# Twelve of 103 zero fills moved from GpSimd's DMA queue to SyncE's in an attention-and-FFN training step

## The chip, the cores and the metric

The kernel runs on one core of one Trainium2 chip. The metric is device time in microseconds (us), the median of several runs.

The engines are PE (matmul), DVE (VectorE), ACT (ScalarE), POOL (GpSimd) and SP (SyncE). SP only issues DMAs here. POOL issues DMAs too, through a queue that the profile calls "software_dynamic"; those of SP and ACT are "hardware_dynamic".

## The reference, cut to what matters

One decoding step and its gradient: layer norm, attention of one query over the last 4096 rows of a 32768-row cache (8 key/value heads), a residual, a second layer norm, a bilinear gated FFN. The outputs are the result and the gradients of all inputs.

```python
W = min(4096, max(256, Sk // 4))              # 4096 of Sk = 32768 rows are used
k = jnp.repeat(k_cache[:, :, Sk - W:, :], rep, axis=1)
v = jnp.repeat(v_cache[:, :, Sk - W:, :], rep, axis=1)
...
g = x @ w_gate;  u = x @ w_up;  h = g * u;  return h @ w_down
...
_out, _vjp = jax.vjp(_f, A_x, A_k_cache, A_v_cache, ...)   # gradients of the whole caches
```

Only 4096 of 32768 rows are used, so seven eighths of the two cache gradients are zeros. They must be written all the same: 224 MiB of zeros. 206 MiB of them are 103 writes of 2 MiB, the "fills" of this text. The other 18 MiB go out on SP's queue late in pass 2 and at the end.

## The kernel before: what the change touches

The kernel has three stages. Pass 1 goes over the eight heads (scores, softmax, moments) and loads K and V. The middle holds the output projection `wo`, the FFN and its gradient, in three blocks of weights. Pass 2 goes over the heads again and writes the gradients of K and V.

The 103 fills go out on POOL's queue. They read one SBUF area, `zeros`. Its upper half is lent to block 1 of the FFN weights in between, and this makes three kinds of fill:

- `HALF0` fills read the full width of `zeros`. Block 1's weights may be loaded only when all of these have finished.
- Fills `HALF0` to `HALF1` read the lower half twice, so they may go on while block 1's weights lie in the upper half.
- The rest must wait until block 1 is done and the upper half has been set to zero again (below called *the memset*).

```python
HALF0, HALF1 = 42, 63
zeros = ar(0, ZW)                              # ZW = 8192 columns, all 128 partitions
wgu_off = [RB + 28 * KB, ZW // 2]              # block 1's w_gate, w_up: upper half of zeros
# ... cut ...
def send_fills(n0, n1, halves=False):
    for reg in fills[n0:n1]:
        if halves:
            ZQ.dma_start(out=reg.rearrange("p (k f) -> p k f", k=2), in_=zeros[:, 0:ZW // 2].unsqueeze(1).to_broadcast([128, 2, ZW // 2]))
        else:
            ZQ.dma_start(out=reg, in_=zeros)

send_fills(0, HALF0)
send_fills(HALF0, HALF1, True)
# ... cut: pass 1, with its loads of K and V ...
after = {0: [("K", 3), ("V", 3)], 1: [("K", 4), ("V", 4), ("K", 5)], 2: [("V", 5)], 3: [("V", 6), ("K", 6)], 4: [("K", 7)], 5: [("V", 7)]}
# ... cut: wo in two halves, load_wo(0) in pass 1, load_wo(1) behind it; then load_block(0), load_block(1) ...
for n in range(len(BLOCKS)):
    # ... cut: the FFN block's compute ...
    if n + 2 < len(BLOCKS):
        load_block(n + 2)
    if n == 1:
        nc.vector.memset(ar(ZW // 2, ZW // 2), 0.0)     # "the memset"
        send_fills(HALF1, len(fills))
```

One thing must be known about the language: the order of instructions on an engine's queue is not the order of the program text. The build reorders them, keeping the dependences. SP's loads of V3, V4 and V5 (V3 is the V of head 3), for example, go out at 26 to 35 us, long before the place where the text has them. `tc.issue_after(x)` pins what it encloses behind `x` on the same engine, but says nothing about how far behind.

## Time and profile before

| | before |
|---|---|
| time, median of 3 runs | 803.09 us (802.88 to 803.20) |
| span of the profiled run | 802.6 us |
| busiest compute engine | PE, 57% of the span |
| moved by DMA | 334.84 MB, mean 417 GB/s |
| pass 1 ends (`wo`'s second half can be issued) | 299.5 us |
| the memset | 375.1 to 376.8 us |
| last compute | 720.6 us |

The page cuts the span into 40 slices. Here are its row of DMA business (in tenths; 9 is 90% or more) and the rate in each slice.

```profile
DMA  9999999999999999999999999999999999999993
GB/s 354 430 430 431 429 428 430 429 429 429 428 424 425 425 419 403 420 423 426 428 421 412 429 430 429 427 428 427 426 425 425 425 425 424 422 408 423 429 438 171
```

The DMA engines have no gap in 39 of 40 slices. The table of windows gives the same in numbers: stretch in us, its length, busy time of each engine with its number of instructions, the granted TensorE clock, the DMA share, GB/s.

```profile
350.00:370.00 20.00, 6.53 (x48) 3.91 (x48) 5.34 (x18) 1.29 (x4) 2.00 (x3) 0.50 1.02 422
370.00:380.00 10.00, 2.03 (x5) 0.57 (x6) 9.48 (x22) 0.00 (x0) 1.33 (x2) 0.50 1.01 428
380.00:390.00 10.00, 3.09 (x20) 2.06 (x19) 7.08 (x13) 2.52 (x5) 1.33 (x2) 0.50 1.01 429
390.00:400.00 10.00, 3.74 (x13) 2.99 (x13) 6.65 (x25) 0.00 (x0) 1.21 (x2) 0.50 1.01 427
...
720.00:770.00 50.00, 0.00 (x0) 0.00 (x0) 0.56 (x1) 0.39 (x1) 0.00 (x0) 0.50 1.01 426
770.00:790.00 20.00, 0.00 (x0) 0.00 (x0) 0.00 (x0) 0.00 (x0) 0.00 (x0) 0.50 0.93 401
790.00:803.00 13.00, 0.00 (x0) 0.00 (x0) 0.00 (x0) 0.00 (x0) 0.00 (x0) 0.50 0.17 74
```

Two readings matter. First, the middle of the kernel, where compute waits most, still has a DMA share of 1.01. Second, the end: after 720 us no compute is left, and in the last 13 us the share is 0.17. The 16 DMA engines do not finish together.

The chain of work that ended last reads thus:

```profile
PE 35%; DMA 32%; DVE 16%; ACT 4%; issue 2%; another core or an unknown queue 0%; SPq 0%; ACTq 0%; DVEq 0%
```

It names PE first, but it follows waits of instructions back from the last one. It can't say that 16 engines were full throughout. The DMA row says it.

SP's own instructions near the end of pass 1, in order of time (start, length; merged instructions of one kind show the time from the first to the end of the last):

```profile
248.13 0.33 SPq L196 DMA_DIRECT2D arena<-in_A_v_cache_dram  x1
260.67 0.57 SPq L352 DMA_DIRECT2D arena<-in_B_w_gate_dram  x1
278.95 0.34 SPq L321 DMA_DIRECT2D arena<-in_A_wo_dram  x1
292.02 1.62 SPq L353 DMA_DIRECT2D arena<-in_B_w_down_dram  x2
299.52 0.33 SPq L321 DMA_DIRECT2D arena<-in_A_wo_dram  x1
300.39 15.55 SPq L351 DMA_DIRECT2D arena<-in_B_w_gate_dram  x2
316.00 1.16 SPq L352 DMA_DIRECT2D arena<-in_B_w_gate_dram  x1
```

V7 is loaded at 248, the two halves of `wo` at 279 and 299.5. Then SP stands still: the second w_gate load in the line at 300.39 is block 1's and waits until 315.4 for the last full-width fill.

### The profile page before, as it was taken

The page shows a single profiled execution, that of the slowest core. Times are in us where ns is not written, and L with a number is a line of the kernel's source. Part 1 is how long each engine was busy: PE and PEld are TensorE (multiplying, and loading weights), DVE is VectorE, ACT ScalarE, POOL GpSimd, SP SyncE. Part 2 cuts the span into 40 slices and gives each one's busy share as a digit, 9 for nine tenths or more (in the row PEclk, how much of TensorE's full clock was granted, in tenths as well). Part 3 has the DMA queues.
Part 4 walks back from the last instruction along what each step waited for, and adds up shares of the span by engine and source line. Part 5 has one row for each costly group of instructions (what it writes and reads, how often), then busy time and mean ns, then how long its engine had stood idle before and what let it go on. Part 6 is the DMA issues. An engine that isn't in the chain of part 4 may idle for free.

```text
span 802.6 us, 8458 instructions
## 1 busy us (share of the span) xinstructions
PE 460.6 (57%) x3157; PEld 247.8 (31%) x3180; DVE 368.5 (46%) x1173; ACT 196.1 (24%) x309; POOL 63.6 (8%) x112
## 2 busy tenths in 40 slices
PE   0469999999999992622329397645263054630000
PEld 0334554545645551311219143322122012200000
DVE  2026264463462652255680876766691175860000
ACT  0143314223224000000002045543341034540000
POOL 4000000010100100011110010000000000000000
PEclk9989999999999997555559689776557557655555
DMA  9999999999999999999999999999999999999993
GB/s 354 430 430 431 429 428 430 429 429 429 428 424 425 425 419 403 420 423 426 428 421 412 429 430 429 427 428 427 426 425 425 425 425 424 422 408 423 429 438 171
DMA packets 29103, 334.84 MB, mean 417 GB/s; under 512 B 2819, under 2 KB 5638, under 8 KB 6918
## 3 DMA queue, kind: packets, MB, share of 16 engines
q0 software_dynamic: 17520, 216.01, 63.7%
q1 hardware_dynamic: 10102, 116.68, 34.7%
q10 hardware_dynamic: 1440, 1.61, 0.6%
q8 instruction: 25, 0.41, 0.2%
q14 instruction: 16, 0.13, 0.0%
HBM read 53.69 MB, written 280.59 MB: 416 GB/s over the span
## 4 chain that ended last, share of the span: by engine, by line
PE 35%; DMA 32%; DVE 16%; ACT 4%; issue 2%; another core or an unknown queue 0%; SPq 0%; ACTq 0%; DVEq 0%
DMA out_dram<-arena 17%; PE M_ps L311 10%; PE ok_ps L315 6%; PE rows_ps L255 6%; PE tr_ps L252 4%; DMA dh_bc<-in_grad_out_dram 4%; DMA arena<-in_A_k_cache_dram 4%; DMA arena<-in_A_wo_dram 3%; ACT arena L269 2%; DVE arena L640 2%; DVE arena L641 2%; DVE arena L452 2%; PE dqb_ps L495 2%; DMA arena<-in_B_w_up_dram 2%; DMA arena<-in_B_w_gate_dram 2%
## 5 line engine op out<-in xcount | busy, mean ns | idle before, releaser
L307 DVE TENSOR_SCALAR arena<-arena,p_f 128x256 bf16<-128x256 bf16 x512 | 109.9, 284 | 66.9 <-PE M_ps L311 35.7
L311 PE MATMUL M_ps<-arena 128*128 128x512 bf16 x489 | 120.1, 380 | 1.4 <-issue 0.2
L255 PE MATMUL rows_ps<-arena,vpad 128*16 128x512 bf16 x256 | 86.0, 430 | 23.3 <-DVE arena L603 16.8
L252 PE MATMUL tr_ps<-ident_bf,arena 128*128 128x128 bf16 x1024 | 88.5, 237 | 15.3 <-DMA arena<-in_A_k_cache_dram 9.5
L252 PEld LDWEIGHTS <-arena 128*128 128x128 bf16 x1024 | 66.3, 105 | 65.5 <-issue 54.9
L132 POOL DMA_DIRECT2D out_dram<-arena x82 | 45.1, 550 | 522.2 <-DMA out_dram<-arena 506.3
L269 ACT COPY arena<-tr_ps 128x1024 bf16<-128x1024 bf16 x64 | 61.8, 1015 | 88.6 <-PE tr_ps L252 88.6
L633 PE MATMUL d_ps<-arena,rT 32*128 32x512 bf16 x256 | 44.4, 507 | 63.1 <-DVE arena L641 37.6
L311 PEld LDWEIGHTS <-arena 128*128 128x128 bf16 x512 | 46.2, 99 | 50.8 <-issue 6.5
L315 PE MATMUL ok_ps<-arena 128*16 128x256 bf16 x512 | 57.5, 273 | 0.9 <-DVE arena L296 0.9
L601 ACT COPY arena<-tr_ps 128x1024 bf16<-128x1024 bf16 x32 | 32.5, 1016 | 97.7 <-PE tr_ps L252 40.4
L637 ACT CAST arena<-d_ps 128x512 bf16<-128x512 f32 x64 | 37.6, 587 | 69.5 <-PE d_ps L633 69.5
L640 DVE CAST arena<-d_ps 128x512 bf16<-128x512 f32 x64 | 44.0, 687 | 14.5 <-PE d_ps L633 14.3
L315 PEld LDWEIGHTS <-arena 128*16 128x16 bf16 x512 | 45.4, 90 | 13.9 <-issue 3.4
L641 DVE CAST arena<-d_ps 128x512 bf16<-128x512 f32 x64 | 43.6, 681 | 7.3 <-DMA out_dram<-arena 7.3
L638 ACT CAST arena<-d_ps 128x512 bf16<-128x512 f32 x64 | 38.1, 595 | 6.8 <-DMA out_dram<-arena 6.8
L633 PEld LDWEIGHTS <-rT 32*128 32x128 bf16 x256 | 11.2, 95 | 90.5 <-issue 58.2
L255 PEld LDWEIGHTS <-vpad 128*16 128x16 bf16 x256 | 19.1, 91 | 56.7 <-issue 49.1
L318 ACT COPY arena<-M_ps 128x512 f32<-128x512 f32 x16 | 8.6, 589 | 75.0 <-PE M_ps L311 75.0
L507 DVE CUSTOM_DVE_ANT_0 arena<-arena 128x4096 bf16<-128x4096 bf16 x3 | 13.1, 4423 | 24.3 <-ACT arena L500 24.3
L603 DVE COPY arena<-tr_ps 128x1024 bf16<-128x1024 bf16 x32 | 21.7, 682 | 3.7 <-PE tr_ps L252 3.7
L130 POOL DMA_DIRECT2D out_dram<-arena x21 | 14.0, 666 | 114.3 <-DMA out_dram<-arena 114.3
(196 smaller groups left out, 368.5 us busy)
## 6 DMA issues: line engine op xcount, KB each, us to landing
out_dram<-arena POOLq DMA_DIRECT2D x103, 2048.0 KB, 55.3
out_dram<-arena SPq DMA_DIRECT2D x18, 2048.0 KB, 33.3
arena<-in_A_v_cache_dram SPq DMA_DIRECT2D x10, 2048.0 KB, 49.9
arena<-in_A_k_cache_dram SPq DMA_DIRECT2D x8, 2048.0 KB, 29.4
out_dram<-arena SPq DMA_DIRECT2D x4, 4096.0 KB, 58.8
arena<-in_A_wq_dram SPq DMA_DIRECT2D x2, 3072.0 KB, 14.8
arena<-in_A_wo_dram SPq DMA_DIRECT2D x2, 1792.0 KB, 17.8
out_dram<-arena SPq DMA_DIRECT2D x2, 1792.0 KB, 32.6
```

The source lines that it names most:

```text
L132: ZQ.dma_start(out=reg, in_=zeros)
L252: nc.tensor.transpose(tr_ps[:, dh, i, :], X_sb[:, 4 * q + i, dh * 128:(dh + 1) * 128], ident_bf[:])
L255: nc.tensor.matmul(rows_ps[:], lhsT=pad[:, dh, 16 * q:16 * q + 16], rhs=XT[:, dh].rearrange("p t k -> p (t k)"), start=(q == 0 and dh == 0 ...
L269: sT_ps = dots(kv_at(K_off[g]), KT_slot, vpad[g % 2], rows1, ps_c, "cols", lambda q, XT, ps: nc.scalar.copy(out=XT, in_=ps))
L307: nc.vector.tensor_scalar(out=pK[:, i, hh, :], in0=K_sb[:, t, :], scalar1=p_f[:, 8 * i + c, hh:hh + 1], scalar2=None, op0=ALU.mult)
L311: nc.tensor.matmul(M_ps[:, vh, :], lhsT=V_sb[:, t, vh * 128:(vh + 1) * 128], rhs=pK[:, i, :, :].rearrange("p h d -> p (h d)"), start=(t == ...
L315: nc.tensor.matmul(ok_ps[:, k, :], lhsT=ppad[g % 2][:, 8 * (t % 4) + t // 4, :], rhs=X_sb[:, t, :], start=(g == 0 and k == 0 and t == 0), ...
L633: nc.tensor.matmul(d_ps[:, qi].rearrange("p w d -> p (w d)"), lhsT=rT[32 * q:32 * (q + 1), :], rhs=RB_[32 * q:32 * (q + 1), l, :], start=T ...
L637: nc.scalar.copy(out=stV[:, t:t + 2, :], in_=d_ps[:, :, 0, :])
L638: nc.scalar.copy(out=stK[:, t:t + 2, :], in_=d_ps[:, :, 1, :])
L640: nc.vector.tensor_copy(out=stV[:, t:t + 2, :], in_=d_ps[:, :, 0, :])
L641: nc.vector.tensor_copy(out=stK[:, t:t + 2, :], in_=d_ps[:, :, 1, :])
```

## The change

The intent, as far as the diff tells it: have the full-width fills done sooner, so that block 1's weights can come sooner, and keep the DMA engines fed by putting single fills into SP's queue behind loads that have slack.

```diff
-HALF0, HALF1 = 42, 63
+HALF0, HALF1 = 32, 46
+SYNC = 12
...
+    own = fills[len(fills) - SYNC:]
+    fills = fills[:len(fills) - SYNC]
+    def fills_behind(ins, n):
+        with tc.issue_after(getattr(ins, "ins", ins)):
+            for _ in range(n):
+                LD.dma_start(out=own.pop(), in_=zeros)
...
         after = {0: [("K", 3), ("V", 3)], ...}
+        behind = {2: 2, 3: 2, 4: 2, 5: 3}
...
+            if g in behind:
+                fills_behind(ins, behind[g])     # ins: the last load of K or V issued for g
...
     def load_block(n):
         for eng, i, wt in ((LD, 0, B_w_gate), (nc.scalar, 1, B_w_up)):
-            (rows 0 to 383, then rows 384 to 447)
+            (rows 384 to 447, then rows 0 to 383; load_block returns SP's last w_gate load)
...
-            if n + 2 < len(BLOCKS):
-                load_block(n + 2)
+            if n == 0:
+                last = load_block(2)
             if n == 1:
                 nc.vector.memset(ar(ZW // 2, ZW // 2), 0.0)
                 send_fills(HALF1, len(fills))
+                fills_behind(last, 3)
```

Fills that may go ahead of the memset: 63 before; 46 on POOL and 9 on SP after, 55 together. Behind it: 40 before; 45 on POOL and 3 on SP after.

More of the change, by code (lines that the diff above doesn't have):

```diff
@@ L195, in load_kv @@
     def load_kv(off, cache, g):
-        LD.dma_start(out=kv_at(off), in_=cache[0, g, Sk - W:, :].rearrange("(p t) d -> p t d", t=T))
+        return LD.dma_start(out=kv_at(off), in_=cache[0, g, Sk - W:, :].rearrange("(p t) d -> p t d", t=T))
     load_kv(K_off[0], A_k_cache, 0)
@@ L332 @@
                 if kind == "K":
-                    load_kv(K_off[n], A_k_cache, n)
+                    ins = load_kv(K_off[n], A_k_cache, n)
                 else:
-                    load_kv(V_off[n], A_v_cache, n)
+                    ins = load_kv(V_off[n], A_v_cache, n)
+            if g in behind:
+                fills_behind(ins, behind[g])
             if g == G - 2:
@@ L350, in load_block @@
         for eng, i, wt in ((LD, 0, B_w_gate), (nc.scalar, 1, B_w_up)):
-            eng.dma_start(out=wgu[:, 0:3, i, :], in_=wt[0:384, :].rearrange("(p c) f -> p c f", c=3)[:, :, f0:f0 + w])
             eng.dma_start(out=wgu[0:DQ, 3, i, :], in_=wt[384:D, f0:f0 + w])
+            ins = eng.dma_start(out=wgu[:, 0:3, i, :], in_=wt[0:384, :].rearrange("(p c) f -> p c f", c=3)[:, :, f0:f0 + w])
+            if eng is LD:
+                last = ins
         LD.dma_start(out=wd, in_=B_w_down[f0:f0 + w, :].rearrange("(p b) n -> p b n", b=nb))
+        return last
     load_block(0)
```

## The prediction

> **What bounds the kernel now.** The DMA engines, from beginning to end. The page's slices show DMA at 9 tenths in 39 of 40 slices, and the table of windows gives a DMA share of 0.99 to 1.02 in every stretch from 5 us to 770 us. 334.84 MB are moved; at the 428 GB/s of the window 20:300 that is 782 us of the 802.6 us span. The other 20 us are the start (221 GB/s in the first 5 us), slower mixed traffic (404 GB/s at 300:320, 416 at 420:450), and the end, where the engines finish one after another (401 GB/s at 770:790, 74 in the last 13 us). No compute engine is busy over 57%, and after 720 us only DMA runs.
>
> **What the change does.** It moves no byte fewer. 63 fills could be sent by GpSimd before the late memset; now 46 can, plus 9 on SyncE: 55. After it: 45 on GpSimd and 3 on SyncE, instead of 40. The Trainium skill, page "DMA: Bandwidth & Descriptors", section "Issuing engines are not separate DMA queues", says that queues of all issuing engines run on the same 16 DMA engines. This trace agrees: GpSimd's fills come every 4.9 to 5.1 us when alone and every 9.7 us beside SyncE's loads, with 428 GB/s either way. So moving fills should buy almost nothing directly. Packets of 16 KB take 618 ns on average in the software queue and 614 ns in SyncE's: on 12 fills of about 5 us, some 0.4 us.
>
> **Indirect effects.**
> 1. Block 1's FFN weights overwrite the upper half of the zeros, so their loads wait for the full-width fills: SyncE waits 13.6 us there, 301.7 to 315.3, and ScalarE's w_up load goes only at 327.7. With 32 + 9 full fills rather than 42, this wait should mostly go; the FFN gets some 10 us shorter.
> 2. V5's load is issued already at 35 us, far ahead of the program's place. The two fills behind it then stand before K3's load, which landed at 122.7, when PE needed it. Two fills at 9.7 us each: K3 lands at about 142, pass 1 ends about 18 us later (near 317 instead of 299.5).
> 3. Net, the late memset comes at about 385 instead of 376.8. By 376.8 the DMA had completed 53.6 fills, by 385 it could have completed 55.3; only 55 exist. So the DMA may run dry for a few us near 385.
>
> Compute ending 10 us later costs nothing; only idle DMA costs: 0 to 5 us, against a gain of about 1 us.
>
> **Prediction.** 802.5 us; 797 to 810 holds it 8 times in 10. Faster by over 2%: 0.02. Within 2%: 0.94. Slower by over 2%: 0.04.
>
> **What would show it.** DMA share still about 1.01 in all windows, except perhaps a dip near 375 to 392; PE idle some 18 us before the scores that need K3 (near 123 us) and pass 1 ending near 317; SyncE's wait for GpSimd's fills before block 1's load shorter than 5 us; last compute between 715 and 740; the end still staggered over some 15 us.
>
> **What would make it wrong.** If the fills run out well before the memset (a longer delay of pass 1, or SyncE's fills holding up the wo and FFN loads), each idle us of DMA costs one us: 15 us or more would make it slower by over 2%. If the staggered end comes from software-issued fills on one slow DMA engine, fewer of them could save up to 5 us. If the fills behind V5 are issued only later, pass 1 is not delayed and nothing runs dry.

## The result, and the profile after

| | before | after |
|---|---|---|
| time, median (4 runs each) | 802.99 us (801.63 to 803.20) | 812.67 us (812.12 to 813.48) |
| span of the profiled run | 802.6 us | 810.3 us |
| pass 1 ends (`wo`'s second half can be issued) | 299.5 us | 319.1 us |
| the memset | 375.1 to 376.8 us | 394.1 to 395.9 us |
| last compute | 720.6 us | 738.6 us |

The ratio is 1.0125, with a 95% interval of 1.0107 to 1.0143. A ratio here is the mean time of one kernel's runs over that of the other's of the same rounds, so it is not quite the ratio of the medians. The change made the kernel 1.2% slower. That is below 2%, but clear of noise, and outside the predicted range (797 to 810 us).

The same rows of the page, after:

```profile
DMA  9999999999999999998499999999999999999997
GB/s 358 427 432 427 429 431 428 430 431 429 428 423 429 411 426 423 419 425 361 180 425 392 426 436 427 425 428 425 422 429 420 426 422 430 421 420 405 439 432 332
```

There is a hole in slices 19 and 20 (361 and 180 GB/s), and the last slice is fuller than before (332 instead of 171 GB/s). The windows:

```profile
350.00:370.00 20.00, 11.78 (x96) 8.18 (x93) 9.50 (x23) 1.80 (x5) 0.00 (x0) 0.58 1.01 425
370.00:380.00 10.00, 2.85 (x8) 0.72 (x8) 4.92 (x16) 1.29 (x4) 0.00 (x0) 0.50 1.02 422
380.00:390.00 10.00, 3.69 (x40) 3.19 (x40) 1.20 (x2) 0.00 (x0) 0.00 (x0) 0.50 0.24 95
390.00:400.00 10.00, 2.02 (x5) 0.56 (x6) 9.48 (x25) 0.87 (x1) 3.62 (x7) 0.50 0.33 131
...
720.00:770.00 50.00, 7.17 (x37) 1.76 (x37) 12.89 (x27) 9.18 (x17) 0.00 (x0) 0.52 1.01 419
770.00:790.00 20.00, 0.00 (x0) 0.00 (x0) 0.00 (x0) 0.00 (x0) 0.00 (x0) 0.50 1.01 432
790.00:800.00 10.00, 0.00 (x0) 0.00 (x0) 0.00 (x0) 0.00 (x0) 0.00 (x0) 0.50 0.99 426
800.00:811.00 11.00, 0.00 (x0) 0.00 (x0) 0.00 (x0) 0.00 (x0) 0.00 (x0) 0.50 0.54 229
```

Between 380 and 400 us the DMA share is 0.24 and 0.33. POOL shows why, in its instructions in order of time:

```profile
342.79 0.67 POOL L131 DMA_DIRECT2D out_dram<-arena  x1 [9.31 <-DMA out_dram<-arena]
396.19 1.08 POOL L133 DMA_DIRECT2D out_dram<-arena  x2 [52.72 <-DVE arena L443]
```

POOL sent the last fill it was allowed at 342.8 and stood still for 52.7 us until the memset (L443 of the changed kernel) was done. What had been queued was finished near 382, but for a few packets.

To put a number on it I took starts and durations of all DMA packets in the trace. At each moment, idle is 16 minus the packets in flight (not below zero), over 16. Summed up to the last packet this is the mean idle time of one DMA engine:

| mean idle per DMA engine, us | start (to 20 us) | middle | end (from 750 us) | sum | span | span minus sum |
|---|---|---|---|---|---|---|
| before | 2.0 | 0.1 | 9.9 | 11.9 | 802.6 | 790.7 |
| after | 2.1 | 14.3 | 2.7 | 19.2 | 810.3 | 791.2 |

The last column is the same within half a microsecond: the fills cost the same DMA time in either queue. The 7.7 us between the spans are 14.3 us more idle in the middle, less 7.1 us that came back at the end; the rest is rounding, the start and that half microsecond. The end is less ragged because in the dry stretch the engines that were behind could catch up: at 384 to 389 us never more than 3 packets of fills were in flight, leftovers of engines that were behind, while the others waited. The landings show it too. Each fill reports its landing in 16 parts, and I take the time from the first part to the last as a measure of how far apart the engines are. It was 11.2 us for the fill that POOL sent at 376.8 in the kernel before, and 0.8 us for its first fill behind the dry stretch after the change. For the last transfer on SP's queue it was 16.4 us before and 5.7 us after.

So two questions are left: why was the memset 19 us later, and is it this lateness, through the dry engines, that cost the time?

**Where the 19 us arise.** PE's list in order of time holds one long wait in pass 1 that the kernel before does not have at that place:

```profile
172.19 1.89 PE L261 MATMUL tr_ps<-ident_bf,arena 128*128 128x128 bf16 x16 [18.40 <-DMA arena<-in_A_k_cache_dram]
```

PE waited 18.4 us for a load of K. Which one, SP's list shows:

```profile
34.61 0.33 SPq L205 DMA_DIRECT2D arena<-in_A_v_cache_dram  x1
90.01 0.33 SPq L205 DMA_DIRECT2D arena<-in_A_k_cache_dram  x1
90.43 0.95 SPq L141 DMA_DIRECT2D out_dram<-arena  x2
91.43 0.60 SPq L205 DMA_DIRECT2D arena<-in_A_v_cache_dram  x1
117.84 3.82 SPq L205 DMA_DIRECT2D arena<-in_A_k_cache_dram  x2
```

The fills pinned "behind V5" (34.61) were put by the build behind K3's load (90.01). K3 still landed at 122.4. The line at 117.84 holds two loads: K5, which goes to the place of V1, at 117.8, and K4, which goes to the place of K1 and had to wait for that, at 121.3. Both stood behind two fills more than before. By the semaphores in the trace K4 landed at 172.2, where PE's wait ends; in the kernel before it landed at 152.2, and PE did not wait for it. SP's queue had been full since the start, at half of the bandwidth, so a 2 MiB fill took some 9.7 us (POOL's fills came every 9.7 us then): two of them, 19.4 us, against 20.0 us by which K4 came later and 18.4 us of PE's wait. The Trainium skill, page "DMA: Bandwidth & Descriptors", section "Queues, rings and completion order", says that on each DMA engine descriptors are consumed in ring order. This trace agrees: what SP issued from 90 us on landed in the order of issue, K3 at 122.4, the fills at 132.6 and 142.7, then a V at 152.6, K5 at 162.4 and K4 at 172.2.

**The FFN was not shortened.** From the end of pass 1 to the memset's start it took 75.6 us before (299.5 to 375.1) and 75.0 us after (319.1 to 394.1). SP again, after:

```profile
267.72 0.34 SPq L205 DMA_DIRECT2D arena<-in_A_v_cache_dram  x1
268.10 4.59 SPq L141 DMA_DIRECT2D out_dram<-arena  x3
280.27 26.15 SPq L363 DMA_DIRECT2D arena<-in_B_w_gate_dram  x2
306.47 1.29 SPq L364 DMA_DIRECT2D arena<-in_B_w_gate_dram  x1
307.87 1.43 SPq L330 DMA_DIRECT2D arena<-in_A_wo_dram  x1
311.63 1.75 SPq L367 DMA_DIRECT2D arena<-in_B_w_down_dram  x2
319.13 0.33 SPq L330 DMA_DIRECT2D arena<-in_A_wo_dram  x1
```

Block 1's w_gate load now stands *ahead* of the first half of `wo`. It waits, until 305.9, for the last full-width fills. These were the three that SP itself had put behind V7: the last of them landed at 305.8, POOL's last full-width fill at 284.3. And `wo` waits behind the load. `wo`'s first half went out at 307.9, 11 us before the end of pass 1; in the kernel before it went out 20.6 us before it. In the projection PE waited for `wo` twice:

```profile
330.24 6.00 PE L391 MATMUL ao_ps<-arena,oX_bf 128*1 128x448 bf16 x16 [8.27 <-DMA arena<-in_A_wo_dram]
345.68 5.12 PE L391 MATMUL ao_ps<-arena,oX_bf 128*1 128x448 bf16 x16 [9.44 <-DMA arena<-in_A_wo_dram]
```

Before, it was once:

```profile
303.49 3.19 PE L376 MATMUL ao_ps<-arena,oX_bf 128*1 128x448 bf16 x16 [1.13 <-DVE oX_bf L373]
320.06 5.76 PE L376 MATMUL ao_ps<-arena,oX_bf 128*1 128x448 bf16 x16 [13.38 <-DMA arena<-in_A_wo_dram]
```

What block 1's earlier weights gained was given back by the later `wo`. The last matmul of the projection ended at 350.8, 31.7 us after the end of pass 1, against 26.3 us before (325.8); from there to the memset it took 43.3 us instead of 49.3. So 5.4 us were lost and 5.9 won.

### The profile page after: what moved, and what is told of

The parts are those of the page before. It is cut to its first block, busy times and chain, and to the rows that moved or that the text cites. A ratio compares the mean times of both kernels' runs of the same rounds, so it can differ in the third digit from the quotient of the medians.

```text
span 810.3 us, 8485 instructions
## 1 busy us (share of the span) xinstructions
PE 463.4 (57%) x3180; PEld 247.5 (31%) x3180; DVE 368.5 (45%) x1173; ACT 196.2 (24%) x309; POOL 55.6 (7%) x100
## 4 chain that ended last, share of the span: by engine, by line
DMA 35%; another core or an unknown queue 26%; DVE 14%; PE 9%; issue 4%; POOL 2%; ACT 1%; SPq 0%; DVEq 0%; ACTq 0%; POOLq 0%
DMA out_dram<-arena 35%; DVE arena L656 3%; DVE arena L657 2%; DVE arena L468 2%; PE dqb_ps L511 2%; PE rows_ps L264 2%; DVE arena L549 1%; DVE arena L642 1%; PE d_ps L649 1%; PE tr_ps L261 1%; POOL out_dram L133 1%; DVE arena L438 1%; DVE arena L523 1%; POOL out_dram L131 1%
## 5 line engine op out<-in xcount | busy, mean ns | idle before, releaser
L320 PE MATMUL M_ps<-arena 128*128 128x512 bf16 x512 | 123.6, 383 | 0.0
L133 POOL DMA_DIRECT2D out_dram<-arena x77 | 41.7, 544 | 516.7 <-DMA out_dram<-arena 463.7
L264 PEld LDWEIGHTS <-vpad 128*16 128x16 bf16 x256 | 18.7, 90 | 57.0 <-issue 49.3
L391 PE MATMUL ao_ps<-arena,oX_bf 128*1 128x448 bf16 x32 | 11.1, 532 | 17.7 <-DMA arena<-in_A_wo_dram 17.7
```

The costliest lines, as they stand in the source:

```text
L264: nc.tensor.matmul(rows_ps[:], lhsT=pad[:, dh, 16 * q:16 * q + 16], rhs=XT[:, dh].rearrange("p t k -> p (t k)"), start=(q == 0 and dh == 0 ...
L320: nc.tensor.matmul(M_ps[:, vh, :], lhsT=V_sb[:, t, vh * 128:(vh + 1) * 128], rhs=pK[:, i, :, :].rearrange("p h d -> p (h d)"), start=(t == ...
```

## The experiments

The theory after reading the trace: the memset is late, the 55 fills run out first, and only the dry DMA engines cost time. Rivals: fills on SP cost as such (1); late compute costs as such (2); 55 fills ahead of the memset are simply too few (3). All seven kernels gave correct results. Two cautions on the expectations. Where they say "K3" of the late load (e1, e3, e5, e6), it was K4. And the "Rival 2" in e1's text is another one: that `wo` behind block 1's load makes the memset late. Each ratio compares with runs of the kernel before in the same rounds.

### e1: the two fills pinned behind V5 given back to POOL

```diff
-HALF0, HALF1 = 32, 46
-SYNC = 12
+HALF0, HALF1 = 34, 48
+SYNC = 10
-        behind = {2: 2, 3: 2, 4: 2, 5: 3}
+        behind = {3: 2, 4: 2, 5: 3}
```

> Theory (the DMA engines run dry because the FFN's memset comes 19 us late, and K3 behind two fills is what makes it late): without the two fills behind V5 (GpSimd sends them, so 55 fills before the memset as in the changed kernel) K3 lands near 123 us, PE does not wait for it, pass 1 ends at 299 to 302 us, the memset ends at 376 to 382 us, when 53.6 to 54.6 of the 55 fills are done; the DMA is dry for 0 to 3 us; 801 to 804 us. Rival 1 (SyncE's fills as such cost, by their packets or by SyncE's waits for completion): 10 of the 12 are still there, so most of the loss stays, 809 us or more. Rival 2 (wo(0) late behind block 1's load is what makes the memset late): memset still 5 us or more later than 377, time above 804.

Measured: 807.51 us, ratio to before 1.0053 (1.0033 to 1.0073). The first half of the theory held: PE's 18.4 us wait is gone, pass 1 ends at 300.6 us. But the memset starts at 389.4 us, only 4.7 us sooner than in the changed kernel, and the engines still run dry:

```profile
380.00:390.00 10.00, 3.25 (x37) 2.92 (x37) 5.51 (x11) 0.00 (x0) 0.00 (x0) 0.50 0.27 116
```

The expected 801 to 804 us was a miss; what came is what e1's own "Rival 2" foresaw (memset 5 us or more late, time above 804). SP's list shows what took over:

```profile
260.85 39.02 SPq L363 DMA_DIRECT2D arena<-in_B_w_gate_dram  x2
299.92 1.38 SPq L364 DMA_DIRECT2D arena<-in_B_w_gate_dram  x1
301.42 1.39 SPq L330 DMA_DIRECT2D arena<-in_A_wo_dram  x1
```

Block 1's load holds SP until 299.4, so `wo`'s first half goes at 301.4, after the end of pass 1. The two delays overlap in the changed kernel: with K4 on time, the wait of `wo` grows instead. K4's delay is one cause, and not enough of it: without it a little under half of the loss is left (0.5% of 1.2%).

### e3: eight more half-width fills allowed ahead of the memset

```diff
-HALF0, HALF1 = 32, 46
+HALF0, HALF1 = 32, 54
```

> The changed kernel, but GpSimd may send 54 fills (not 46) before the memset, so 63 in all as before; after it 37. Theory: K3 and pass 1 stay 19 us late, memset at 394 to 400 us, but the DMA is never dry (57.5 fills could be done by 396, 63 exist): 801 to 804 us, end staggered over 14 to 17 us as before. Rival 2 (late compute as such pushes the end out): 810 to 813 us, since compute is as late as in the changed kernel. Rival 1 (SyncE's fills as such): 810 to 813 us.

Measured: 802.35 us, ratio 0.9984 (0.9962 to 1.0007). Compute is as late as in the changed kernel: pass 1 ends at 320.1 us, the memset starts at 394.9, the last compute ends at 740.3 us. SP's 12 fills are all there. Yet the whole loss is gone, and so is the dry stretch:

```profile
380.00:390.00 10.00, 3.68 (x40) 3.18 (x40) 0.42 (x2) 0.00 (x0) 1.33 (x2) 0.50 1.02 425
390.00:400.00 10.00, 2.03 (x5) 0.57 (x6) 9.48 (x22) 0.10 (x1) 1.08 (x2) 0.50 1.01 429
```

This is the run that decides: rivals 1 and 2 fall. Neither fills on SP nor late compute cost anything by themselves that the interval would show.

### e4: the kernel before, with 55 instead of 63 fills ahead of the memset

```diff
-HALF0, HALF1 = 42, 63
+HALF0, HALF1 = 42, 55
```

> The kernel before, only with 55 instead of 63 fills allowed ahead of the memset; no fill on SyncE. Theory: memset near 377 us as before, 53.6 fills done by then, so dry for 0 to 3 us: 801 to 804 us. If a lower count of early fills alone costs (rival 3), near 812 us.

Measured: 803.17 us, ratio 0.9998 (0.9976 to 1.0020), mean idle in the middle 0.05 us. The memset starts at 375.0. Rival 3 falls: 55 fills are enough if the memset comes then.

### e6: the kernel before, starved on purpose

```diff
-HALF0, HALF1 = 42, 63
+HALF0, HALF1 = 42, 48
```

> The kernel before with 48 fills ahead of the memset: starved on purpose, without any fill on SyncE or any late K3. Theory: fills run out near 346 us; block 2's loads, then alone on the engines, land in some 4 us instead of 15, so the memset comes at 362 to 368 us; dry for 12 to 18 us on the mean of the 16 engines; the staggered end shrinks by about 7 us as in the changed kernel; so 807 to 815 us. If dry time is not what costs, 802 to 804 us.

Measured: 822.62 us, ratio 1.0242 (1.0222 to 1.0261). The engines were dry for 18.7 us on the mean and the end shrank to 3.4 us of idle; the memset started at 364.7. One of the dry windows:

```profile
360.00:370.00 10.00, 2.03 (x5) 0.57 (x6) 9.48 (x22) 0.34 (x1) 3.28 (x7) 0.50 0.26 105
```

So starvation alone, without any fill on SP, slows the kernel. But the time is 8 us above the expected range: a miss in size. Idle accounts for 12.1 of the 18.0 us between the profiled spans (sum of idle 24.0 against 11.9). Another 4 us lie behind the last packet: in this kernel POOL's queue is the last to finish, and the program ended 5.4 us after its last packet, against 1.5 us in the kernel before, where SP's is the last. Why POOL's takes longer was not tried, and 2 us are unexplained.

### e5: block 1's loads put behind `wo` again, the fills behind V5 left in place

```diff
-    load_wo(1)
+    wo1 = load_wo(1)                       # load_wo returns its instruction
     load_block(0)
-    load_block(1)
+    with tc.issue_after(wo1.ins):
+        load_block(1)
```

> The changed kernel, but block 1's SyncE loads are put behind wo(1), the order that the kernel before has; the two fills behind V5 stay. Theory (two causes, one after the other: K3 late by 19 us, and wo(0) held up on SyncE's queue by block 1's load, which waits for the full-width fills): pass 1 still ends near 320 us; wo(0) issued near 299 instead of 308; FFN from the end of pass 1 to the memset 70 to 76 us instead of 74 to 75, so the memset starts at 389 to 394; dry for 8 to 14 us; 807 to 812 us. If K3 were irrelevant and the order alone the cause: 801 to 804 us.

Measured: 803.19 us, ratio 0.9985 (0.9966 to 1.0003). Pass 1 is still late (319.6 us), but `wo`'s first half goes at 299.1, PE's first wait for it is gone and the second is 6.1 us. From the end of pass 1 to the memset it takes 65.2 us (319.6 to 384.8), 10.4 us less than in the kernel before. The memset came 4 us sooner than expected, so the time missed the expected 807 to 812. It fell into the band that the expectation gives to a rival, "the order alone the cause" (801 to 804). And indeed, with the order put right, the late K4 costs nothing that can be measured, while K4 put right alone (e1) leaves 0.5%. The late `wo` is thus the larger of the two causes, and K4's delay costs time only together with it. The engines do run dry, for a shorter time:

```profile
380.00:390.00 10.00, 2.02 (x5) 0.57 (x6) 9.48 (x22) 0.23 (x1) 3.08 (x6) 0.50 0.52 215
...
790.00:801.00 11.00, 0.00 (x0) 0.00 (x0) 0.00 (x0) 0.00 (x0) 0.00 (x0) 0.50 0.60 256
```

A share of 0.52 in one window of 10 us is 4.8 us of mean idle, and it cost nothing. The end has 2.8 us of idle instead of 9.9. An engine that is ahead and waits in the middle waits less at the end; only when the engines that are *behind* have to wait is time lost (the gaps below the last table measure it).

### e7: both undone, ten fills left on SP

```diff
-HALF0, HALF1 = 32, 46
-SYNC = 12
+HALF0, HALF1 = 34, 48
+SYNC = 10
-        behind = {2: 2, 3: 2, 4: 2, 5: 3}
+        behind = {3: 2, 4: 2, 5: 3}
     (and load_block(1) behind load_wo(1), as in e5)
```

> Both undone: no fill behind V5 (GpSimd sends those two) and block 1's loads behind wo(1). 10 of the 12 fills stay on SyncE, 55 fills ahead of the memset as in the changed kernel. Theory: pass 1 ends at 300 to 302, wo(0) issued near 280, memset starts at 370 to 380 us, the engines are dry for at most 2 us, 801 to 804 us, the end staggered again (mean idle 8 to 10 us there). If SyncE's fills as such cost, or 55 fills are too few beside them, 806 us or more.

Measured: 801.25 us (801.10 to 801.59), ratio 0.9958 (0.9941 to 0.9975). `wo`'s first half is issued at 280.9, the memset starts at 371.2, nothing runs dry:

```profile
370.00:380.00 10.00, 4.42 (x23) 2.53 (x24) 7.91 (x21) 1.55 (x3) 2.64 (x5) 0.50 1.02 433
380.00:390.00 10.00, 1.31 (x5) 0.66 (x4) 7.71 (x17) 0.97 (x3) 0.53 (x1) 0.50 1.00 426
```

It is the fastest kernel, 0.4% below the kernel before of the same rounds. These runs of the kernel before scattered more than usual (802.87 to 805.81 us), so I would not build on the size.

### e8: only the number of full-width fills cut, no fill on SP

```diff
-HALF0, HALF1 = 42, 63
+HALF0, HALF1 = 32, 63
```

> The kernel before with only the number of full-width fills cut from 42 to 32 (63 ahead of the memset as before, no fill on SyncE): the change's aim for block 1's weights alone. SyncE's order at build puts block 1's w_gate load ahead of wo(0), as in the changed kernel. Full-width fills are done by about 260 us, so that load does not wait for them. Theory: the FFN is shorter by 5 to 12 us (memset starts at 363 to 371), and the time is still 801 to 804 us, since the DMA engines were busy anyway. If a shorter FFN is worth its time, 791 to 798 us.

Measured: 802.09 us, ratio 0.9970 (0.9955 to 0.9985). The memset starts at 362.9 us, 12.2 us sooner than in the kernel before: the FFN did become shorter, and it brought no more than the 0.3% in the ratio. The run also shows where SP's new order comes from. The build puts block 1's w_gate load (250.1 and 251.2 us here) ahead of `wo` (280.1) with `HALF0` at 32, without the swap of the two row ranges and without SP's fills. Here it does no harm, because the 32 full-width fills are done by then (the last landed at 248.2). In the changed kernel, nine more full-width fills, on SP, made that load wait.

### What the seven runs say together

Mean idle per DMA engine in us, from the packets of each profiled run, and the profiled span:

| kernel | pass 1 ends | memset starts | fills ahead | idle middle | idle end | all idle | span | median time |
|---|---|---|---|---|---|---|---|---|
| before | 299.5 | 375.1 | 63 | 0.1 | 9.9 | 11.9 | 802.6 | 802.99 |
| after | 319.1 | 394.1 | 55 | 14.3 | 2.7 | 19.2 | 810.3 | 812.67 |
| e1 no fills behind V5 | 300.6 | 389.4 | 55 | 9.3 | 2.8 | 14.1 | 805.8 | 807.51 |
| e5 `wo` first | 319.6 | 384.8 | 55 | 4.8 | 2.8 | 9.5 | 801.0 | 803.19 |
| e7 both | 301.5 | 371.2 | 55 | 0.0 | 8.0 | 10.1 | 799.8 | 801.25 |
| e3 eight more fills | 320.1 | 394.9 | 63 | 0.1 | 10.1 | 12.2 | 801.4 | 802.35 |
| e4 before, 55 fills | 301.6 | 375.0 | 55 | 0.1 | 8.9 | 11.0 | 800.8 | 803.17 |
| e8 before, HALF0 32 | 300.7 | 362.9 | 63 | 0.1 | 7.5 | 9.6 | 800.3 | 802.09 |
| e6 before, 48 fills | 301.2 | 364.7 | 48 | 18.7 | 3.4 | 24.0 | 820.6 | 822.62 |

(For e1 the column "pass 1 ends" holds the start of the copy of pass 1's results, since the load of `wo` went out later there for the other reason. Elsewhere that copy starts 0.9 us after the time given. The median times stem from different rounds: the ratios above are the fair comparison.) Span minus all idle is 789.2 to 791.7 us for all but e6 (796.6), which has the extra end described above. So in no variant did the transfers themselves take longer, and the spans differ by idle time, to within some 2.5 us.

Which idle time counts can be read from the packets too. In the changed kernel the last leftover ends at 388.5 us and the next packet starts at 396.8: for 8.3 us nothing at all is in flight. In e1 this gap is 3.4 us, in e6 12.8 us; in e5 and all the others there is none. Against the kernel before, the span is 7.7 us longer in the changed kernel, 3.2 in e1 and 18.0 in e6 (3.9 of them behind the last packet), and 1.6 shorter in e5. It is the time in which even the engines that were behind had nothing to do that made the kernels slower, and not the mean.

## Why the prediction was wrong, point by point

- **"The DMA engines, from beginning to end" bound the kernel: right.** e3 and e8 move compute by 20 us later and 12 us sooner and change the time by 0.3% at most.
- **Moving fills between the queues buys almost nothing directly: right.** Span minus idle is 790.7 before and 791.2 after. The section "Issuing engines are not separate DMA queues" of the skill's page on DMA agrees.
- **Step 2, pass 1 late by about 18 us, ending near 317: right in size (319.1), wrong in the load.** I took K3, on the belief that the fills would be issued right behind V5 at 35 us. They went out at 90 us, behind K3; the late load was K4 (PE waited 18.4 us, until 172.2). That the size still fits is partly luck: two fills stood ahead of a needed load, but of another one.
- **Step 1, "the FFN gets some 10 us shorter", failed.** This is the step that made the prediction wrong. The wait that I expected to vanish, 13.6 us, became a wait of 25 us (280.9 to 305.9), and, what counts more, it moved ahead of `wo` on SP's in-order queue. The FFN took 75.0 us instead of 75.6. With the old order (e5) it took 65.2 us: the gain I had predicted was there, but it was cancelled by the later `wo`. The step's own reason did not hold either: "32 + 9 full fills rather than 42" is one fill fewer, and the last of the nine was issued only at 270.9 and landed at 305.8, when POOL's 32 had been done for 21 us. I had not asked when the last of SP's fills would land, nor where in the queue the load that waits for it would stand. (Under "What would make it wrong" the prediction does name fills on SyncE that hold up the loads of `wo` and the FFN, but the forecast left them out.)
- **Step 3, "late memset at about 385", followed from step 1:** it was done at 395.9. The count of fills was right: I put the moment when 55 fills would be done just before 385, and the engines ran dry near 382. With a memset at 385 the dry stretch would have been short, as e5 shows: 4.8 us, and 803.19 us of time, close to the predicted 802.5.
- **"Each idle us of DMA costs one us": wrong.** The first 5 us or so cost nothing (e5), because the engines were out of step and the end became less ragged; 14.3 us cost 7.7 us of span, close to the 8.3 us in which no packet was in flight. Had the rule been right, the change would have cost 14 us.
- **"The end still staggered over some 15 us": wrong,** for the same reason: 2.7 us of mean idle at the end instead of 9.9.

What stays open: which DMA engine lags, and why, since the records do not name engines; and the 2 us of e6 above.

## What to carry to other kernels

In a kernel like this one, whose DMA engines are full from beginning to end, a change is worth only the DMA idle time that it removes or makes, and of that only what the engine that finishes last feels; so count, at every point where a supply of background transfers can be cut off, how many are left and when the next may start. A transfer put into an in-order queue delays everything behind it, and a load that must wait for such transfers blocks its whole queue: before pinning anything, look at the built order and ask what stands behind the one that waits. A background queue that runs out within a few us of its refill may still be free, if the engines are out of step (4.8 us of mean idle in e5); one that leaves them dry for 14.3 us on the mean was not.

## What the Trainium skill lacked or had wrong

- Page "DMA: Bandwidth & Descriptors", section "Where 436 GB/s comes from", says that the HBM side, about 358 GB/s for one core, binds transfers between HBM and SBUF. This core, running alone, moved 428 GB/s between SBUF and HBM in the window from 20 to 300 us, reads and writes mixed, near the 435 GB/s that the same page gives as the ceiling of the fabric. (Elsewhere the page ties 358 to both cores of a pair streaming, and the section itself calls a single core's 425 GB/s near the rate of the fabric. So it is this one sentence that needs the condition, and not the figure that is wrong.) The measurement decides: 358 was not the limit here.
- The page on DMA notes that two of the engines are usually slower in traces, but not what uneven progress costs in a kernel that keeps all 16 full: here 7.5 to 10.1 us of mean idle time per engine at the end when nothing ran dry, 2.7 to 3.4 us when a dry stretch near the middle had let the slow ones catch up.
- The page on DMA says that an engine serves the descriptors of a ring in order, and it does not draw the consequence for a producer: two fills of 2 MiB ahead of a load delayed it by 20.0 us, and one load waiting for fills held the issue of the next for 25 us.
- No page tells how the end of a program depends on the queue that finishes last: the program ended 1.2 to 1.5 us after its last packet when SP's queue was the last to finish, and 5.4 us after it when POOL's was (e6, one profiled run).
